# A new instruction order for three fused networks: first weight units in halves, fewer warm-up products, the passage to the third network opened

## The chip, the cores and the metric

The kernel runs on one core of a Trainium2 chip. The core has a matrix engine (TensorE, PE in the rows; PEld is its loading of the stationary operand), a vector engine (DVE), an activation engine (ACT), a general engine (POOL) and a queue for transfers (SP), each with its own instruction stream. They wait for each other by semaphores. The metric is the device time of one execution in microseconds, lower is better.

## The reference

Three networks follow each other. Everything is float32 with the weights given as 64-bit floats; B = 4, 8 heads, 576 positions, width 64.

```python
def _attn_ref(q, k, v):                       # landmark attention, m = 32
    q_lm = q.reshape(B, H, m, S // m, D).mean(axis=3)
    k_lm = k.reshape(B, H, m, S // m, D).mean(axis=3)
    A, Bm, C = sm(q, k_lm), sm(q_lm, k_lm), sm(q_lm, k)
    Z = Bm.T / (norm1(Bm) * norminf(Bm) + 1e-6)
    for _ in range(6):
        Z = 2 * Z - Z @ Bm @ Z
    return A @ Z @ C @ v
def _moe_ref(x, w1, w2, w3, w_out):           # 2304 tokens, 512 -> 1024 -> 1024 -> 512
    return ((x @ w1) * (x @ w2) @ w3) @ w_out
def _moe2_ref(x, w_in, w_out):                # 512 -> 2048 -> 512
    h = x @ w_in
    return (h * tanh(softplus(h))) @ w_out    # Mish
```

## The kernel before

**Attention** makes, for each of the four batches, landmark sums (DVE), small row-tiled score products on TensorE (32 or 64 rows of the array at a time, in one bank several side by side), the softmaxes and an iterated inverse.

**Second network.** w3 and w_out stand behind each other without anything between, so their product is made once, at the start: 16 units of w3 times 8 units of w_out, 64 products of two fp32 instructions each (line L349, "mm n x" is product x of unit w3n; it needs unit wo j of w_out with j = 2 (n % 4) + x // 2). A unit is 512 KB of 64-bit floats. Its load (L202) is issued on SP; then "da" takes the upper bits on ACT or DVE (L194, L196) and "db" joins them with the rest on DVE (L206), which gives 32-bit numbers. The other matmuls of the two networks are split into a high and a low part and done as three products each (`mm3`, L186 to L188). w1 and w2 are first multiplied with the landmark part ("m b s", L795, small products into the two-bank tile `pair`), and the result is split by ACT and DVE into M ("mh", "ml"). "xa" and "xb" are the two large products with it, six matmuls of 288 columns each, "xm" their product on DVE. Then "sh" and "sl" split the hidden rows into hs, "y u m" multiplies them with the made w3 times w_out, 24 matmuls of 288 columns, and "ye u m" copies the result out of its bank on ACT.

**Third network.** It runs in steps g = 0 to 23, each with a Strassen-like scheme of seven products, "Z0 g" to "Z6 g", six matmuls of 384 columns each into two banks in turn. They need the input y in several sums ("yh", "yl": high part by ACT, low part by DVE) and w_in in several sums ("zs" on DVE, "zh" on ACT, "zl" on DVE; stored by "zd"). S (L1293, ACT) copies Z0's bank, Q, R, C21, C22 and C12 (L1273, DVE) add up, E1, E2 and E3 are the Mish function on ACT in two forms (L1269, L1270), L1 to L3 the low part (DVE), and O0 to O3 the products with w_out. "wh", "wl" and "ws" split a unit of w_out for that and store it. "db 14", "wh 6" belong to unit 14, which is part 6 of w_out. The first use of the Mish function needs its table on ACT, one load (L1269).

**The order.** Nothing is scheduled by a program: the string `ORDER` lists every step by name (with @ENGINE where there is a choice), and `issue` walks through it and emits each step. So the order of the names is the order of the instructions on each engine, and a step waits behind everything ahead of it on its engine. A step's list of needed steps is only used to check the order and its slots; the semaphores come from the tiles that are read and written. Buffers are taken from pools (`raw`, `raw2` for the loaded units, the banks of PSUM in pool "w"). From g = 10 on the steps are emitted by loops that the change doesn't touch.

**Start.** Twenty products of a tile of ones with itself (L1395) go ahead of the string; they compute nothing that is used. L1273 to L1293 are in `z_ops`; L202 to L206 are `load`, `top_bits` and `join`.

Of the kernel before, what the change touches and what calls it, by code (L numbers as in the profile page):

```python
# [18 lines left out]
SPIN = 20  # L19
# [137 lines left out]
def kernel(  # L157
# [43 lines left out]
    def load(w, n):  # L201
        nc.sync.dma_start(out=w.bitcast(U16)[:, 1:2049], in_=wts[n].bitcast(U16))  # L202
# [75 lines left out]
    def got(key):  # L278
        pool, i = at[key]
        return pools[pool][i]  # L280
# [1194 lines left out]
```

## Time and profile before

| what | value |
|---|---|
| time, median of 3 runs | 706.01 us (705.64 to 706.74) |
| the profiled execution | 706.82 us |
| its span in the trace | 705.0 us |
| TensorE busy | 697.4 us, 5004 matmuls |
| VectorE (DVE) busy | 395.2 us |
| ScalarE (ACT) busy | 281.6 us |
| granted clock of TensorE | 1.00 |

The span is the time from the first to the last recorded instruction; the profiled execution's own time has 1.8 us around it. Busy times are sums of durations on one engine. Matmuls overlap, so the duration of one is longer than the distance to the next; where a price per matmul is needed it is the distance.

### The profile page before, as it was taken

The numbers are of one execution on the slowest core, as the hardware profiler recorded it, in microseconds if no ns is written. First come the engines' busy times: TensorE is split into PE (matmuls) and PEld (weight loads), VectorE is DVE, ScalarE is ACT, GpSimd is POOL, SyncE is SP. The second block draws the span as 40 slices with busy tenths as digits, with TensorE's granted clock in tenths as the row PEclk, the third lists the DMA queues.
The fourth block names the chain that finished last, engine by engine and source line by source line (L and its number), as shares of the span: only waits on it lengthen the run. The fifth ranks groups of instructions, "written<-read, shape, count | busy, mean of one in ns | idle before, by whom it ended". The sixth has DMA issues, their size and how long they took to land.

```text
span 705.0 us, 12344 instructions
## 1 busy us (share of the span) xinstructions
PE 697.4 (99%) x5004; PEld 594.3 (84%) x5004; DVE 395.2 (56%) x814; ACT 281.6 (40%) x644; POOL 27.8 (4%) x27
## 2 busy tenths in 40 slices
PE   9999999999999999999999999999999999999997
PEld 4445588888998999999898989898989988989896
DVE  5899787966446435766668667442234544222322
ACT  1355555536344326455454345522222442222222
POOL 0123011111000000000000000000000000000000
PEclk9999999999999999999999999999999999999999
DMA  9987895544042443554483766867544456555302
GB/s 352 383 293 258 267 343 183 171 150 120 17 150 80 153 172 120 195 208 170 151 323 136 274 232 275 299 236 285 210 186 165 165 213 219 204 214 207 152 2 89
DMA packets 36217, 141.38 MB, mean 201 GB/s; under 512 B 3648, under 2 KB 4032, under 8 KB 32576
## 3 DMA queue, kind: packets, MB, share of 16 engines
q1 hardware_dynamic: 36016, 140.46, 55.4%
q8 instruction: 39, 0.64, 0.4%
q14 instruction: 18, 0.15, 0.1%
q10 hardware_dynamic: 144, 0.13, 0.1%
HBM read 106.50 MB, written 34.08 MB: 199 GB/s over the span
## 4 chain that ended last, share of the span: by engine, by line
PE 97%; DVE 1%; ACT 1%; issue 0%; ACTq 0%
PE ps L186 27%; PE ps L187 27%; PE ps L188 27%; PE ps L349 8%; PE pair L795 2%; PE ps L604 1%; PE ps L410 1%; PE pair L1395 1%; PE ps L536 1%; PE ps L515 1%; ACT M L210 0%; DVE M L224 0%; PE pair L410 0%; DVE yH L224 0%; PE ps L517 0%
## 5 line engine op out<-in xcount | busy, mean ns | idle before, releaser
L187 PE MATMUL ps<-hs,W 128*128 128x288 f32 (+1 forms) x298 | 92.3, 310 | 0.0
L186 PE MATMUL ps<-hs,W 128*128 128x288 f32 (+1 forms) x298 | 92.3, 310 | 0.0
L188 PE MATMUL ps<-hs,W 128*128 128x288 f32 (+1 forms) x298 | 92.2, 309 | 0.0
L1273 DVE TENSOR_TENSOR hsb<-ps,zt 128x384 f32<-128x384 f32 x72 | 39.9, 557 | 86.7 <-PE ps L188 86.5
L1269 ACT ACTIVATE hsb<-hsb 128x768 f32<-128x768 f32 (+1 forms) x48 | 32.8, 684 | 114.8 <-DVE hsb L1273 114.8
L186 PE MATMUL ps<-AT,M 128*128 128x288 f32 x256 | 77.7, 304 | 0.1
L188 PE MATMUL ps<-AT,M 128*128 128x288 f32 x256 | 75.4, 295 | 0.0
L187 PE MATMUL ps<-AT,M 128*128 128x288 f32 x256 | 75.4, 294 | 0.0
L1273 DVE TENSOR_TENSOR zt<-ps,zt 128x384 f32<-128x384 f32 x48 | 26.7, 556 | 81.9 <-PE ps L188 76.5
L224 DVE TENSOR_TENSOR W<-hsb,W 128x384 fp32r<-128x384 f32 (+1 forms) x72 | 49.2, 687 | 17.4 <-ACT W L1270 17.4
L349 PE MATMUL ps<-wo,raw 128*128 128x512 f32 x128 | 58.5, 603 | 0.0
L188 PEld LDWEIGHTS ps<-hs,W 128*128 128x128 f32 x298 | 55.9, 188 | 1.8
L187 PEld LDWEIGHTS ps<-hs,W 128*128 128x128 f32 x298 | 56.1, 188 | 1.3
L186 PEld LDWEIGHTS ps<-hs,W 128*128 128x128 f32 x298 | 56.0, 188 | 1.3
L186 PEld LDWEIGHTS ps<-AT,M 128*128 128x128 f32 x256 | 48.0, 188 | 9.6 <-issue 5.0
L187 PEld LDWEIGHTS ps<-AT,M 128*128 128x128 f32 x256 | 48.1, 188 | 0.0
L188 PEld LDWEIGHTS ps<-AT,M 128*128 128x128 f32 x256 | 48.0, 188 | 0.0
L349 PEld LDWEIGHTS ps<-wo,raw 128*128 128x128 f32 x128 | 24.0, 196 | 25.4 <-issue 20.2
L210 ACT ACTIVATE a<-ps 128x288 f32<-128x288 f32 x64 | 25.6, 410 | 45.7 <-PE ps L188 45.4
L833 DVE TENSOR_TENSOR h<-a,ps 128x288 f32<-128x288 f32 x64 | 28.1, 450 | 26.0 <-ACT hs L210 9.8
L187 PE MATMUL ps<-yH,zw 128*128 128x384 f32 x120 | 40.3, 336 | 0.3 <-DVE yH L224 0.3
L187 PE MATMUL ps<-yH,hs 128*128 128x384 f32 x120 | 40.2, 335 | 0.0
(196 smaller groups left out, 1542.9 us busy)
## 6 DMA issues: line engine op xcount, KB each, us to landing
raw<-in_wts_dram SPq DMA_DIRECT2D x72, 512.0 KB, 4.6
zw<-zd SPq DMA_DIRECT2D x8, 1792.0 KB, 7.6
hs<-zd SPq DMA_DIRECT2D x8, 1792.0 KB, 7.3
zd<-zw SPq DMA_DIRECT2D x4, 1792.0 KB, 7.2
zd<-hs SPq DMA_DIRECT2D x4, 1792.0 KB, 7.5
wy<-wod SPq DMA_DIRECT2D x12, 512.0 KB, 6.7
W<-wod SPq DMA_DIRECT2D x10, 512.0 KB, 7.1
k<-in_kT_dram SPq DMA_DIRECT2D x8, 576.0 KB, 5.7
```

The costliest lines, as they stand in the source:

```text
L186: T.matmul(out=o, lhsT=lh, rhs=rh, start=first, stop=False, skip_group_check=partial)
L187: T.matmul(out=o, lhsT=lh, rhs=rl, start=False, stop=False, skip_group_check=partial)
L188: T.matmul(out=o, lhsT=ll, rhs=rh, start=False, stop=last, skip_group_check=partial)
L210: S.activation(o, x, ACTF.Copy)
L224: (G if e == "POOL" else V).tensor_tensor(o, x, f32(hi), op=ALU.subtract)
L349: T.matmul(out=got(f"acc{i}"), lhsT=f32(middle(got(f"w3{n}"))[:, o:o + 128]), rhs=WO0[j // 4][:, j % 4], start=j == 0, stop=j == 7)
L410: T.matmul(out=mine(f"{key}{g}{hf}")[32 * i:32 * i + 32, 0:HALF], lhsT=st[lm][r, p, :], rhs=st[x][r, p, hf * HALF:(hf + 1) * HALF], start= ...
L515: T.transpose(out=mine(f"ct{g}0")[:, ck * 128:(ck + 1) * 128], in_=x[:, ck * 128:(ck + 1) * 128], identity=idn)
L795: T.matmul(out=got("p" + key)[32 * i:32 * i + 32, c, :], lhsT=LT[r, b, 2 * c + par, :], rhs=w12(f"w{bp}{s}{2 * c + par}")[r], start=True, ...
L833: V.tensor_tensor(hslice(u, s), got("s" + key), got("b" + key)[:, 0:HALF], op=ALU.mult)
L1269: S.activation(e, src_, ACTF.Mish)
L1273: V.tensor_tensor(o, x, y, op=ALU.add)
```

## The change

Five fewer warm-up products. Units w30 and w34 of w3 are loaded, and decoded, in two halves of 256 columns each, and a product waits for its half only. Z0 of g = 0 may stand ahead of the last y products (its wait for all of them is taken out of the list; S gets the wait for all xm, and C and E of g = 0 get the wait for all y). The string `ORDER` is another one throughout.

```diff
-SPIN = 20
+SPIN = 15
+
+HALVED = (0, 4)
...
-    "ld wo0,da wo0@ACT,db wo0,ld w34,da w34@DVE,ld w30,da w30@ACT,db w34,mm 4 0,mm 4 1,db w30,mm 0 1,ld wo1,da wo1@DVE,db wo1,"
...
+    "ld w34a,ld wo0,da wo0@ACT,ld w30a,db wo0,dA w30a@DVE,ld w30b,dA w30b@DVE,dB w30a,mm 0 0,dB w30b,ld wo1,mm 0 1,"
...
-    def top_bits(e, w, u):
-        o, i = u.bitcast(F16).rearrange("p (n w) -> p n w", w=2)[..., 1], w.bitcast(BF16)[:, 2:2050].rearrange("p (n w) -> p n w", w=4)[..., 2]
+    def top_bits(e, w, u, c=slice(0, 512)):
+        o, i = u.bitcast(F16).rearrange("p (n w) -> p n w", w=2)[:, c, 1], w.bitcast(BF16)[:, 2:2050].rearrange("p (n w) -> p n w", w=4)[:, c, 2]
...
-    def load(w, n):
-        nc.sync.dma_start(out=w.bitcast(U16)[:, 1:2049], in_=wts[n].bitcast(U16))
+    def load(w, n, c=slice(0, 512)):
+        a, z = 4 * c.start, 4 * c.stop
+        nc.sync.dma_start(out=w.bitcast(U16)[:, 1 + a:1 + z], in_=wts[n].bitcast(U16)[:, a:z])
...
+    def decode_halves(u, n, raw, take):
+        for i, h in enumerate("ab"):
+            c = slice(256 * i, 256 * i + 256)
+            step(f"ld {u}{h}", "SP", [f"ld {u}a"], lambda e, c=c: load(raw(), n, c), take if i == 0 else ())
+            step(f"dA {u}{h}", ("ACT", "DVE"), [f"ld {u}{h}"] + ([f"dA {u}a"] if i else []), lambda e, c=c: top_bits(e, raw(), got("u" + u), c),
+                 () if i else {"u" + u: "u"})
+            step(f"dB {u}{h}", "DVE", [f"dA {u}{h}"], lambda e, c=c: join(raw(), got("u" + u), None, c), (), ["u" + u])
...
-        step(me, "PE", [f"db w3{n}", f"db wo{j}"] + chain(f"mm{i}", me), mm,
+        step(me, "PE", [f"dB w3{n}{'ab'[a]}" if n in HALVED else f"db w3{n}", f"db wo{j}"] + chain(f"mm{i}", me), mm,
...
+    all_xm = [f"xm {b} {s} {h}" for b in (2, 3) for s in range(NS) for h in range(2)]
...
-            ("Z0", "PE", z_wait(0, f"C12 {p}", *all_y), lambda e: z_mm(g, 0)),
-            ("S", "ACT", [f"Z0 {g}", f"C21 {p}"], lambda e: S.activation(zt(0), z_bank(0), ACTF.Copy)),
+            ("Z0", "PE", z_wait(0, f"C12 {p}"), lambda e: z_mm(g, 0)),
+            ("S", "ACT", [f"Z0 {g}", f"C21 {p}"] + all_xm, lambda e: S.activation(zt(0), z_bank(0), ACTF.Copy)),
...
-        return [(f"{n} {p if n[0] == 'O' else g}", e, w, fn) for n, e, w, fn in table]
+        first = all_y if g == 0 else []
+        return [(f"{n} {p if n[0] == 'O' else g}", e, w + first * (n[0] in "CE"), fn) for n, e, w, fn in table]
```

The transfer queue SP at the start of the program, before: raw is the landing place of a unit, 128x2048 a whole one (16-bit columns), k and q a half of a batch's keys or queries, idn the identity matrix. By `ORDER` the first units are wo0, w34, w30, wo1, w31, wo2, w35, wo3.

```order
L202 DMA raw_73<-in_wts_dram 128x2048 x3
L202 DMA raw<-in_wts_dram 128x2048 x4
L202 DMA raw_73<-in_wts_dram 128x2048
L386 DMA k<-in_kT_dram 128x2x576 x2
L386 DMA q<-in_qT_dram 128x2x576 x2
L324 DMA idn<-in_ident_dram 128x128
L202 DMA raw_73<-in_wts_dram 128x2048 x3
```

And after the change, where the units are w34a, wo0, w30a, w30b, wo1, w34b, wo2, w31, w35, wo3, and after q and k w32, wo4 and w36:

```order
L206 DMA raw_73<-in_wts_dram 128x1024
L206 DMA raw_73<-in_wts_dram 128x2048
L206 DMA raw_73<-in_wts_dram 128x1024 x2
L206 DMA raw<-in_wts_dram 128x2048
L206 DMA raw_73<-in_wts_dram 128x1024
L206 DMA raw<-in_wts_dram 128x2048 x3
L206 DMA raw_73<-in_wts_dram 128x2048
L398 DMA q<-in_qT_dram 128x2x576
L398 DMA k<-in_kT_dram 128x2x576 x2
L398 DMA q<-in_qT_dram 128x2x576
L206 DMA raw_73<-in_wts_dram 128x2048 x3
```

Half a unit now stands ahead of wo0, the four halves of q and k come in another sequence, and the identity matrix is loaded later; w32 and wo4 still follow right behind q and k.

ACT at the passage from y to Z, before: y<-ps is ye (the copy of a y product out of its bank), yW and yH are yh, zt<-ps_78 is S 0, and the last two rows are E1 0. [waits PE_49] marks a wait for TensorE.

```order
L210 ACTIVATE y_3126<-ps_81 128x288
L210 ACTIVATE yH_3539<-sums 128x768 [waits Activation_49]
L210 ACTIVATE y_3432<-ps_2867 128x288 [waits PE_49]
L210 ACTIVATE yW_3546<-y_2140 128x768 [waits DMAHW7_49,DMAHW3_49,Activation_49]
L210 ACTIVATE yH_3575<-sums 128x768 [waits DVE_49,Activation_49]
L210 ACTIVATE y_3432<-ps_2866 128x288 [waits PE_49]
L210 ACTIVATE yW_3583<-y_2140 128x768 [waits DMAHW1_49,DMAHW0_49,Activation_49]
L210 ACTIVATE y_3432<-ps_77 128x288
L1293 ACTIVATE zt<-ps_78 128x384 [waits PE_49]
L1269 ACT_TABLE_LOAD
L1269 ACTIVATE hsb<-ps_78 128x384 [waits PE_49]
L1270 ACTIVATE W_64<-ps_78 128x384
```

And after: S 0 is the first row, y_3457<-ps_82 in the fourth is ye 7 3, the two hs<-sums are zh6 1 and zh4 1, W_65<-raw is wh 6, and the two y behind it ye 7 2 and ye 7 1.

```order
L1306 ACTIVATE zt<-ps_78 128x384 [waits PE_49]
L214 ACTIVATE yW_3529<-y_2151 128x768 [waits DMAHW7_49,DMAHW0_49,Activation_49]
L214 ACTIVATE y_3149<-ps_81 128x288
L214 ACTIVATE y_3457<-ps_82 128x288 [waits PE_49]
L214 ACTIVATE hs_1953<-sums 128x256 [waits DVE_49]
L214 ACTIVATE hs_1953<-sums 128x256
L214 ACTIVATE W_65<-raw 128x512 [waits DMAHW1_49,DVE_49]
L214 ACTIVATE y_3457<-ps_79 128x288
L214 ACTIVATE y_3457<-ps_77 128x288
L1282 ACT_TABLE_LOAD
L1282 ACTIVATE hsb<-ps_78 128x384 [waits PE_49]
L1283 ACTIVATE W_64<-ps_78 128x384
```

Before, the table's load follows S 0 directly. After, eight rows lie between the two, among them ye 7 3. On TensorE, Z0 0 now stands between y 7 0 and y 7 1, and Z1 0 to Z3 0 follow y 7 3, then Z4 0.

## Rows read from the trace of the kernel before

**Rows 1.** The page: span, and busy time of each engine.

```profile
span 705.0 us, 12344 instructions
...
PE 697.4 (99%) x5004; PEld 594.3 (84%) x5004; DVE 395.2 (56%) x814; ACT 281.6 (40%) x644; POOL 27.8 (4%) x27
```

**Rows 2.** Waits of TensorE: engine, line, releaser, us in total, times, longest.

```profile
PE pair L1395 <- DVE ones L1393: 1.5, 1, 1.5
PE ps L186 <- DVE hsb L1273: 0.7, 1, 0.7
...
PE pair L795 <- DVE M L224: 0.5, 2, 0.3
```

**Rows 3.** Windows: us, busy time (instructions) per engine, TensorE clock, DMA share, GB/s.

```profile
20.00:40.00 20.00, 20.00 (x118) 8.72 (x119) 18.28 (x39) 10.01 (x24) 3.70 (x3) 1.00 0.96 356
250.00:300.00 50.00, 50.00 (x377) 50.00 (x376) 29.43 (x67) 22.98 (x59) 0.00 (x0) 1.00 0.45 153
```

**Rows 4.** Timeline of the start: start us, us, engine, line, operation, idle before, releaser.

```profile
4.36 0.78 ACT L194 ACTIVATE top<-raw 128x512 f16<-128x512 bf16 x1 [2.35 <-DMA raw<-in_wts_dram]
...
5.17 0.69 DVE L206 SCALAR_TENSOR_TENSOR wo<-raw,top 128x512 int32<-128x512 int32 x1 [3.77 <-ACT top L194]
...
5.70 1.91 PEld L1395 LDWEIGHTS <-ones 128*128 128x128 bf16 x9 [0.28 <-issue]
5.78 0.45 DVE L196 TENSOR_SCALAR top<-raw 128x512 f16<-128x512 bf16 x1
...
7.45 0.78 ACT L194 ACTIVATE top<-raw 128x512 f16<-128x512 bf16 x1 [2.32 <-DMA raw<-in_wts_dram]
...
7.93 11.37 PE L349 MATMUL ps<-wo,raw 128*128 128x512 f32 x26
...
21.41 0.78 ACT L194 ACTIVATE top<-raw 128x512 f16<-128x512 bf16 x1 [13.17 <-DMA raw<-in_wts_dram]
...
22.68 0.79 ACT L194 ACTIVATE top<-raw 128x512 f16<-128x512 bf16 x1 [0.49 <-DMA raw<-in_wts_dram]
...
23.53 0.68 DVE L206 SCALAR_TENSOR_TENSOR wo<-raw,top 128x512 int32<-128x512 int32 x1
...
24.26 0.31 PEld L349 LDWEIGHTS ps<-wo,raw 128*128 128x128 f32 x2 [0.69 <-DVE wo L206]
```

**Rows 5.** Chain of waits, 58 to 70 us: start us, us, what.

```profile
60.82 1.92 PE ps L349 x4
...
62.99 5.36 PE ps L349 x12
```

**Rows 6.** Chain of waits, 118 to 123.5 us.

```profile
121.15 0.61 ACT M L210
...
121.78 0.70 DVE M L224
...
122.52 1.04 PE pair L795 x9
```

**Rows 7.** Timeline of the passage from y to Z.

```profile
321.34 0.41 ACT L210 ACTIVATE y<-ps 128x288 f32<-128x288 f32 x1 [1.32 <-PE ps L188]
...
321.64 0.84 ACT L210 ACTIVATE yW<-y 128x768 fp32r<-128x768 f32 x1
...
324.34 0.34 PE L186 MATMUL ps<-yW,zw 128*128 128x384 f32 x1
...
325.58 0.49 ACT L1293 ACTIVATE zt<-ps 128x384 f32<-128x384 f32 x1 [2.80 <-PE ps L188]
...
326.09 1.28 ACT L1269 ACT_TABLE_LOAD   x1
...
327.67 0.49 ACT L1269 ACTIVATE hsb<-ps 128x384 f32<-128x384 f32 x1 [0.29 <-PE ps L188]
...
328.59 0.19 PEld L186 LDWEIGHTS ps<-yH,zw 128*128 128x128 f32 x1 [0.23 <-ACT W L1270]
```

**Rows 8.** Groups of ACT by form: busy us, mean ns, idle before, releasers.

```profile
L210 ACT ACTIVATE W<-raw 128x512 fp32r<-128x512 f32 x3 | 2.0, 665 | 6.0 <-DVE raw L206 6.0
```

More of the change, by code (lines that the diff above doesn't have):

```diff
@@ L199, in middle, with join @@
         return w[:, 1:1025].rearrange("p (n w) -> p n w", w=2)[..., 0]
-    def load(w, n):
-        nc.sync.dma_start(out=w.bitcast(U16)[:, 1:2049], in_=wts[n].bitcast(U16))
-    def join(w, u, to=None):
+    def load(w, n, c=slice(0, 512)):
+        a, z = 4 * c.start, 4 * c.stop
+        nc.sync.dma_start(out=w.bitcast(U16)[:, 1 + a:1 + z], in_=wts[n].bitcast(U16)[:, a:z])
+    def join(w, u, to=None, c=slice(0, 512)):
         to = middle(w) if to is None else to.bitcast(I32)
-        V.scalar_tensor_tensor(to, middle(w), 13, u, op0=ALU.logical_shift_right, op1=ALU.bitwise_or)
+        V.scalar_tensor_tensor(to[:, c], middle(w)[:, c], 13, u[:, c], op0=ALU.logical_shift_right, op1=ALU.bitwise_or)
     def copy(e, o, x):
@@ L337, in add_w3 @@
         u = f"w3{n}"
-        decode(u, 8 + n, lambda: got(u), {u: raw_pool(u)})
+        (decode_halves if n in HALVED else decode)(u, 8 + n, lambda: got(u), {u: raw_pool(u)})
         for i in range(4):
```

245 rows, old and new, of the table ORDER are left out of this document.

## The prediction

> **What bounds the kernel now.** I read the busy shares first, then the waits of TensorE, then stretches of the start, of the middle and of the places that the new order rewrites. The reader is to see that TensorE is busy 697.4 of 705.0 us [rows 1], that its waits are few and short (1.5 us before the warm-up, then tenths) [rows 2], and that it runs without a gap at full clock both while the weights are loaded and in the middle of the kernel: 20.00 of 20.00 us busy between 20 and 40 us, 50.00 of 50.00 between 250 and 300 us with 377 matmuls, .133 us each for 288 columns [rows 3]. So the time is a fixed number of matmuls plus the places where TensorE stands still or changes its kind of product. An edit counts only if it removes matmuls, removes such a place or makes a new one. The other engines have 40 to 56% and matter only where TensorE ends up waiting for them.
>
> **The base of the sum.** The profiled execution took 706.82 us, 1.8 us more than its span of 705.0. The sum is made against it. It lies .8 us above the median of the runs, 706.01; I carry the sum over to the median as a difference.
>
> **Start: fewer spins, halves, new order of loads.** The last spins stand .21 us apart (nine loads in 1.91 us [rows 4]), so five fewer free TensorE 1.06 us earlier, at 6.87 us instead of 7.93 [rows 4]. Whether the first product is ready then is a walk along the loads. Two units of 512 KB are decoded 1.27 us apart when their decoding waits for the transfers (21.41 and 22.68 [rows 4]), and the stream stays that full (DMA .96 [rows 3]). In the kernel before wo0 stands first in the queue and its decoding starts at 4.36. Now half a unit, w34a, stands ahead of it, so it starts at 4.36 + .64 = 5.00; ACT takes .78, DVE's join .69, which ends at 6.50. DVE's queue then holds the upper bits of w30a and of w30b and then the join of w30a. A decoding of 128x256 is not in the trace: it lies between half and the whole of .45 and .69 [rows 4]. Three of them end between 7.3 and 8.1; I take 7.6, nearer the half, since these shapes are paid by columns elsewhere. The first product starts at about 7.6 instead of 7.93, and TensorE waits .7 us behind its last spin. The product mm 0 2 then needs wo1, with 3.5 units to its end in the queue: the third unit's decoding started at 7.45 before [rows 4], so wo1's starts at about 8.1, its join ends at 9.7, two products (.86 us each) end at 9.3, and .4 us of the gain is given back.
>
> What decides the start is the end of it. In both kernels 16 products can be made before one needs wo4, and in both ten units and four halves of q and k lead up to wo4 in the queue. Before, ACT decodes it at 22.68, DVE joins it at 23.53, and TensorE's load waits for that until 24.26 [rows 4]. The new kernel has the same bytes ahead of it (the small identity matrix is moved behind, some tenths), the same two steps on the same engines, and comes there some tenths earlier only to wait. I take 0. Bounds: -1.1 (all of the five spins is kept, because other products lie ready) and +.7 (the small transfers or the halves' decoding hold wo1 or wo4 up).
>
> A rule of the Trainium skill speaks against the halves. The row first: back-to-back units of 512 KB come 1.27 us apart [rows 4], about 410 GB/s, so transfers of that size already fill the stream. The page DMA: Bandwidth & Descriptors, section Bandwidth, asks for at least 1 MiB per transfer to have 75% of the peak and gives 341 GB/s for 1 MB. By that rule units and halves alike would be slow; the row disagrees for a queue with many transfers in flight, no row shows 256 KB on loads, and by the rule the sum would move by the four halves, at most to the +.7 that the bound has anyway.
>
> **Changes of the kind of product.** Between plain products stand groups of small row-tiled ones (scores, landmark products, the m products). What such an island costs beyond its own matmuls is read from two pieces of the chain: four w3 instructions behind a group take 1.92 us, twelve behind another 5.36 [rows 5]. The slope is 3.44/8 = .43 each, and the rest, 1.92 - 4 x .43 = .20, belongs to the change out of the group and back. In the program order of TensorE I count 30 such islands before and 26 after. Four times .20 is -.8; the new order makes some other changes more often (transposes next to small products), for which I give back .2: -.6, between -.8 and -.2.
>
> **Waits for the M tiles.** TensorE's m products wait twice for DVE's M, .5 us in sum [rows 2]: m 1 2 at 122.52 us, and m 3 2 later, each time behind the chain ACT M, DVE M, ACT M, DVE M (.61 and .70 each, and TensorE .04 behind it [rows 6]), because too few x products stand between. That chain is about 2.7 us long (twice .61 and .70, and the gaps). In the new order m 1 2 has four more x products and a bp ahead of it (some 3.5 us) and m 3 2 has eight x products instead of four, so both chains end before TensorE arrives: -.5, between -.8 and 0, the zero for a wait that reappears at another m.
>
> **The passage from y to Z.** This is the largest term, and it is a loss. Before, y 7 3 is followed by Z0 at 324.34, S on ACT runs at 325.58, the Mish table is loaded at 326.09 for 1.28 us, E1 starts at 327.67 and Z4, which waits for the bank that E1 reads, at 328.59 [rows 7]. A Z product is six matmuls of 384 columns, .174 each by the .133 of 288 columns [rows 3]; four of them from 324.34 end at 328.52, so Z4 loses .07. The table is hidden, since ACT has nothing else to do there.
>
> In the new order Z0 0 stands ahead of y 7 1, S 0 is early, but the table isn't: ACT's queue has ye 7 3, which waits for y 7 3's end (call it T0), and behind it zh6 1, zh4 1, wh 6, ye 7 2, ye 7 1 and only then the table. ye 7 3 starts at T0 + .20 (S stands .20 behind Z0's six matmuls [rows 7]). Copies of this size follow each other in .30 (321.34, 321.64 [rows 7]) though each lasts .41; wh 6 copies 128x512, .665 us [rows 8], .56 with the same overlap. Five times .30 and .56 are 2.06: table at T0 + 2.26, E1 at T0 + 3.54, and Z4 .92 behind E1's start as before (327.67 to 328.59): T0 + 4.46. TensorE has only Z1, Z2, Z3 to do in that time, 18 x .174 = 3.13. It waits 1.33, less the .07 of before: +1.3. With whole durations (.41, .665) the queue takes 2.7 and the loss is +1.9; with another .30 between the table and E1, as the rows allow (327.67 - 326.09 is 1.58), +2.2. The other end is -.1: ACT's six copies run before T0, or the table early. I take +1.3. Nothing behind it gives it back: Z0 1 already waits for the end of a chain that starts with Z6, and moves with it.
>
> The Trainium skill makes more of the table. The page ScalarE: Activation LUTs, section What ACT_TABLE_LOAD costs, has 1283 ns and another 1380 ns of drain, 2.66 us for each switch. The trace agrees with the first and not with the second: E1 starts 1.58 us after the load's start [rows 7], and there it waited for TensorE. By the rule Z4 would lose another 1.3 us and the sum would be +1.5.
>
> **Everything else** keeps its instructions: the Strassen-like products, the O products and the tail. The longest wait in there, .7 us for hsb at L1273 [rows 2], has the same neighbours. 0, plus or minus .5 for single fetch stalls.
>
> **Sum.** 0 - .6 - .5 + 1.3 + 0 = +.2: 707.0 for an execution like the profiled one, 706.2 for a median like 706.01. A difference under .2% (1.4 us) can't be told from none in this kernel; so the forecast is no change.
>
> **Rivals.**
> - The table costs nothing (the passage is neutral): Z4's bank is free otherwise, or ACT runs the six copies while y 7 3 still computes. For it: ACT is idle most of that stretch. Against it: ye 7 3 reads what y 7 3 writes and stands first. +.2 - 1.3 = -1.1: 704.9.
> - The five spins are won whole: for it, TensorE waits nowhere else between 20 and 40 us [rows 3], so an earlier start might be kept if the products behind 24 us are not bound by loads. Against it, the wait at 24.26. -1.1 more: 705.1. With the first rival too: 703.8.
> - Slower: unit 14 is late. wh 6 stands before the table and needs unit 14 joined on DVE, whose load was only issued behind the stores ws 5 and ws 3 in SP's queue, and which DVE decodes (.45 and .69) behind other differences. It decides from the point where the join ends later than T0 + 1.1 (ACT's turn for wh 6); from there each microsecond is paid in full, since table, E1 and Z4 stand behind it. At T0 + 3 it costs 1.9: 708.1. Against it: y 7 1 to y 7 3 give some 9.6 us for the load.
> - The first weights starve TensorE (halves cost as much as wholes): +.7 to +1, 707.0.
> - The table holds ACT longer than its row: if ACT needed as long again behind the load (1.28) before E1 can run, Z4 would lose another 1.3: 707.5. Against it, E1 runs .30 behind the load's end at 327.37 [rows 7]. That is the drain that the Trainium skill's page ScalarE: Activation LUTs speaks of.
>
> **Chances.** Forecast .50 (705.2 to 707.2 of its own), table free .14, spins kept .11, both .05, unit 14 late .10, starved start .06, table held longer .04. Faster by over .2% (under 704.6): both, about two fifths of the two single gains, and the forecast's lower tail: .26. Slower (over 707.4): most of unit 14, the table held longer, a part of the starved start and the forecast's upper tail: .18. The rest, .56, within. The range of 8 in 10 reaches to 703.9, nearly the two gains together, and to 707.8, short of the late unit.
>
> **What would show it.** First product at 7.5 to 7.7 and the product with wo4 at 24.2 to 24.3, or earlier (then the spins are won). No wait at m 1 2 and m 3 2. The table's load starts 2.2 us after the last matmul of y 7 3, and TensorE waits 1.2 to 1.6 us ahead of Z4, released by ACT W. If the load starts earlier, or Z4 doesn't wait, the first rival holds; if ACT waits for DVE's raw ahead of wh 6, the third. It is wrong if the time moves by over 1.4 us, or if the rest of the body, which I set at 0, has gained or lost more than half a microsecond.

## The result and the profile after

The changed kernel takes 714.22 us (median of 5 runs, 713.93 to 716.82) against 706.01 (705.43 to 706.74): a ratio of 1.0124, with 95% interval 1.0105 to 1.0143 (the ratios here and below are taken over all fast runs and not from the medians, so they differ a little from the medians' quotient). It is slower by 8.2 us. The prediction, 706.2 us with a range of 703.9 to 707.8, was wrong. The profiled execution took 714.84 us, 8.0 more than that of before.

The page of the changed kernel, to be read against [rows 1]: span, and busy time of each engine.

```profile
span 713.0 us, 12348 instructions
...
PE 699.3 (98%) x4999; PEld 594.8 (83%) x4999; DVE 394.6 (55%) x812; ACT 285.7 (40%) x651; POOL 26.0 (4%) x25
```

TensorE has five matmuls fewer, the spins, and is busy 1.9 us longer. So idle time is not the whole loss: some matmuls became slower. The waits of TensorE after the change stand against [rows 2] (engine, tile, line, releaser, us in total, times, longest):

```profile
PE ps L548 <- issue: 2.8, 1, 2.8
PE ps L361 <- DVE raw L210: 1.9, 2, 1.5
PE ps L189 <- ACT W L1283: 1.3, 1, 1.3
PE ps L189 <- DVE hsb L1286: 0.7, 1, 0.7
PE ps L189 <- DVE csm L520: 0.5, 1, 0.5
PE ps L189 <- DVE h L845: 0.3, 1, 0.3
PE ps L616 <- DVE py L673: 0.2, 1, 0.2
```

The two waits for M are gone. New at the top is one of 2.8 us with no releaser but "issue": TensorE waited for nothing that the profile shows. The kernel before has one wait of this kind, which is much shorter:

```profile
PE ps L410 <- issue: 0.6, 1, 0.6
```

The row of 1.3 us is Z4 waiting for ACT. The lines are renumbered: L349 is now L361, L186 to L188 are L189 to L191, L206 is L210, L1273 is L1286, L1269 is L1282.

**Where the 8 us lie.** Two instructions that exist in both kernels, the load for the product with wo4 and that of Z4, cut the span in three. TensorE's busy time between them is from the windows of both traces.

| stretch | before | after | difference |
|---|---|---|---|
| to the product with wo4 | 24.26 | 25.58 | +1.3 |
| from there to Z4 0 | 304.33, busy 302.95 | 311.31, busy 305.58 | +4.4 idle, +2.6 busy |
| from Z4 0 to the end | 376.4 | 376.1 | -0.3 |

The windows of the middle stretch, before and after (us, busy time and instructions of PE, PEld, DVE, ACT, POOL, then clock, DMA share, GB/s):

```profile
24.26:328.59 304.33, 302.95 (x3057) 251.39 (x3057) 208.05 (x474) 145.84 (x387) 26.62 (x22) 1.00 0.54 183
25.58:336.89 311.31, 305.58 (x3056) 252.50 (x3056) 207.79 (x472) 148.28 (x395) 24.86 (x20) 0.99 0.51 176
```

The idle 4.4 us are the stall (2.8, against .6 of the same kind before), the gap at Z4 (1.45 against .08 by the distance of the matmuls' starts; the row of 1.3 counts from the end of the last one), and small waits that came for those that went. Of the 2.6 us busy, 1.8 are worked out below; .8 I could not place.

**The start.** Two pieces of the timeline (start us, us, engine, line, operation, idle before with its releaser), against [rows 4].

```profile
5.40 0.77 ACT L197 ACTIVATE top<-raw 128x512 f16<-128x512 bf16 x1 [3.39 <-DMA raw<-in_wts_dram]
...
7.52 0.31 DVE L199 TENSOR_SCALAR top<-raw 128x256 f16<-128x256 bf16 x1 [0.61 <-DMA raw<-in_wts_dram]
...
8.39 0.75 DVE L210 SCALAR_TENSOR_TENSOR raw<-raw,top 128x256 int32<-128x256 int32 x2
8.87 0.31 PEld L361 LDWEIGHTS ps<-wo,raw 128*128 128x128 f32 x2 [2.03 <-DVE raw L210]
...
23.92 0.79 ACT L197 ACTIVATE top<-raw 128x512 f16<-128x512 bf16 x1 [0.47 <-DMA raw<-in_wts_dram]
...
25.58 0.31 PEld L361 LDWEIGHTS ps<-wo,raw 128*128 128x128 f32 x2 [0.40 <-DVE wo L210]
```

The first product starts at 8.87 us, not at 7.93 as before nor at the 7.6 that was worked out. Its wait is for transfers: w30a's decoding starts at 7.52, although 256 KB and 512 KB stood ahead of it and wo0's decoding had started at 5.40. The whole stream is then behind: wo4's decoding starts at 23.92 instead of 22.68. This place differs between executions: in nine profiled ones with the new start (this one, e1, e2, e3, e5, e7, e8, e9, e13 below) the product with wo4 starts at 24.73 to 25.58, mean 25.11, and in six with the old start (before, e6, e10, e11, e12, e14) at 23.90 to 24.88, mean 24.31. So the start costs about .8 on average, and 1.3 between the two executions compared here. The first product starts at 7.70 to 8.87 (mean 8.32) in the nine and at 7.38 to 8.69 (mean 8.04) in the six, so the five spins less don't bring it forward.

**The stall and what follows it.** Windows of the changed kernel, and the chain of waits there.

```profile
60.00:64.00 4.00, 3.85 (x140) 2.26 (x141) 3.51 (x9) 2.67 (x9) 2.99 (x3) 1.00 1.02 360
64.00:67.00 3.00, 0.25 (x5) 0.16 (x4) 2.93 (x8) 0.00 (x0) 0.48 (x1) 1.00 0.69 276
67.00:70.00 3.00, 3.00 (x7) 1.49 (x6) 1.29 (x6) 2.91 (x11) 0.00 (x0) 0.65 0.04 10
70.00:73.00 3.00, 3.00 (x25) 1.26 (x24) 2.90 (x9) 0.86 (x3) 0.00 (x0) 0.78 0.00 0
68.00:71.00 3.00, 3.00 (x5) 1.31 (x4) 1.93 (x7) 2.72 (x10) 0.00 (x0) 0.50 0.00 0
```

```profile
63.14 0.82 PE ps L548 x36
63.96 2.79 issue
66.75 0.30 PE ps L548 x4
67.05 5.34 PE ps L361 x8
```

TensorE stops in the middle of a group of 40 small products (L548, "cv"), so no operand is missing: 36 of the same group had just run. Ahead of the stop stand 140 matmuls in 4 us (13 in the four before); the new order puts five groups of small ones (16, 40, 32, 16 and 40) in a row. Behind it the granted clock averages .65 and then .78 in windows of 3 us. These are no levels of their own: from 68 to 71 us it is .50, the lower of the two levels (1.2 and 2.4 GHz), and the averages mix it with 1.00, the upper one. The eight w3 matmuls there take 5.34 us. At the .43 of [rows 5] and one change of kind, .1, they would take 3.55: 1.8 us for the clock.

The page's row of the queue that carries instructions (packets, MB, share), then the data queue's row from 60.3 to 63.9 us, where the instruction queue has none, and the instruction queue's from 63.9 to 66.8:

```profile
q8 instruction: 39, 0.64, 0.4%
```

```profile
q1 hardware_dynamic: 532, 1.29, 97.9%
```

```profile
q8 instruction: 1, 0.02, 2.1%
```

39 transfers of 16,384 bytes fit the 10,000 instructions of TensorE, 256 to a block: a matmul and its load are two, so a block lasts 128 matmuls. At .43 us each that is 55 us; the small ones use it up in 3.7 us (from 60.26, which is 256 instructions ahead of the stop, to 63.96). From 60.3 to 63.9 no block came, while the data transfers filled the engines to 97.9%; the next one started at 64.30, 4.0 us after the block before it was used up, and TensorE went on 1.5 us after its end. The Trainium skill's page Runtime: NRT & Kernel Launch, section Instruction fetch mechanics, names such a FIFO with blocks of 16 KiB that the sequencer fetches on a queue of its own, and calls the cost of a crossing "mostly hidden". The size agrees with the row of 39 packets; that it is hidden does not hold here, with 2.79 us.

That such a stop is a wait for instructions is also shown by its place. Counted over all kept traces there are 21 stops over .15 us with no releaser but "issue" in the middle of the kernel, in both orders, with either start and in the joins below. Each stands behind the 961st, the 1473rd or the 1729th recorded instruction of TensorE, which are 512 and 256 apart, whatever product is there; and each ends 1.2 to 1.6 us after the end of a block's transfer. The kernel before has 109 small products in a row at 57.5 us, less than a block, and doesn't stop there; its stop of .6 us is behind the 1473rd instruction, in a run of 229.

**The passage from y to Z**, the chain of waits of the changed kernel against [rows 7]:

```profile
332.48 0.03 ACT y L214
...
332.79 0.71 ACT hs L214 x2
333.50 0.56 ACT W L214
334.06 0.60 ACT y L214 x2
...
334.68 1.28 ACT L1282
...
335.97 0.49 ACT hsb L1282
...
336.89 0.45 PE ps L189
```

TensorE goes on from y 7 3 to Z1 at 332.29, the T0 of the prediction's sum. ye 7 3 starts .19 us later (.20 was worked out), the table's load 2.39 (2.26) and Z4 4.60 (4.46). This term was right step by step; the .13 are the two copies to hs, .71 instead of .60. E1 starts 1.29 us behind the start of the load of 1.28, and it had nothing else to wait for, since Z2 was long done. So no drain of 1.38 us follows the load, which the Trainium skill's page ScalarE: Activation LUTs, section What ACT_TABLE_LOAD costs, adds to it.

### The profile page after: what moved, and what is told of

It reads as the page before. It is cut to its first block, busy times and chain, and to the rows that moved or that the text cites. A ratio compares the mean times of both kernels' runs of the same rounds, so it can differ in the third digit from the quotient of the medians.

```text
span 713.0 us, 12348 instructions
## 1 busy us (share of the span) xinstructions
PE 699.3 (98%) x4999; PEld 594.8 (83%) x4999; DVE 394.6 (55%) x812; ACT 285.7 (40%) x651; POOL 26.0 (4%) x25
## 4 chain that ended last, share of the span: by engine, by line
PE 91%; DMA 3%; DVE 2%; ACT 2%; issue 1%; SPq 1%; ACTq 0%; DVEq 0%
PE ps L189 27%; PE ps L191 27%; PE ps L190 27%; PE ps L361 5%; DMA raw<-in_wts_dram 3%; PE pair L807 2%; PE ps L616 1%; PE ps L422 1%; PE ps L548 1%; SPq L206 1%; DVE raw L210 1%; PE ps L527 0%; DVE M L228 0%; ACT M L214 0%; DVE mx L443 0%
## 5 line engine op out<-in xcount | busy, mean ns | idle before, releaser
L189 PE MATMUL ps<-hs,W 128*128 128x288 f32 (+1 forms) x298 | 92.5, 310 | 0.0
L191 PE MATMUL ps<-hs,W 128*128 128x288 f32 (+1 forms) x298 | 92.2, 310 | 0.0
L1286 DVE TENSOR_TENSOR hsb<-ps,zt 128x384 f32<-128x384 f32 x72 | 39.7, 556 | 86.0 <-PE ps L191 86.0
L1282 ACT ACTIVATE hsb<-hsb 128x768 f32<-128x768 f32 (+1 forms) x48 | 32.9, 685 | 120.6 <-DVE hsb L1286 120.6
L189 PE MATMUL ps<-AT,M 128*128 128x288 f32 x256 | 78.1, 305 | 1.0 <-DVE csm L520 0.5
L191 PE MATMUL ps<-AT,M 128*128 128x288 f32 x256 | 75.6, 295 | 0.0
L1286 DVE TENSOR_TENSOR zt<-ps,zt 128x384 f32<-128x384 f32 x48 | 26.7, 556 | 73.1 <-PE ps L191 70.5
L361 PE MATMUL ps<-wo,raw 128*128 128x512 f32 x128 | 59.7, 616 | 2.5 <-DVE raw L210 1.9
L189 PEld LDWEIGHTS ps<-hs,W 128*128 128x128 f32 x298 | 56.1, 188 | 3.0 <-ACT a L214 0.8
L191 PEld LDWEIGHTS ps<-hs,W 128*128 128x128 f32 x298 | 56.0, 188 | 1.7
L189 PEld LDWEIGHTS ps<-AT,M 128*128 128x128 f32 x256 | 48.1, 188 | 9.3 <-issue 5.4
L361 PEld LDWEIGHTS ps<-wo,raw 128*128 128x128 f32 x128 | 24.7, 201 | 31.7 <-issue 23.2
L191 PEld LDWEIGHTS ps<-AT,M 128*128 128x128 f32 x256 | 48.1, 188 | 0.2 <-DVE M L228 0.2
L197 ACT ACTIVATE top<-raw 128x512 f16<-128x512 bf16 x38 | 29.3, 785 | 34.5 <-DMA raw<-in_wts_dram 30.1
```

Of the source, the lines that this page charges most:

```text
L189: T.matmul(out=o, lhsT=lh, rhs=rh, start=first, stop=False, skip_group_check=partial)
L191: T.matmul(out=o, lhsT=ll, rhs=rh, start=False, stop=last, skip_group_check=partial)
L197: S.activation(o, i, ACTF.Copy)
L361: T.matmul(out=got(f"acc{i}"), lhsT=f32(middle(got(f"w3{n}"))[:, o:o + 128]), rhs=WO0[j // 4][:, j % 4], start=j == 0, stop=j == 7)
L1282: S.activation(e, src_, ACTF.Mish)
L1286: V.tensor_tensor(o, x, y, op=ALU.add)
```

## Experiments

Four kinds: on the stall, on the start, on the passage, and joins of the two orders. "Before" in each batch lay between 705.95 and 706.70 us.

### The stall of the instruction stream

**e2_spread** puts plain products between the groups of small ones.

```diff
-... cs1 1, cm01 1, ... cex01 1, mm 12 0, mm 12 2, mm 12 1, ...
+... cs1 1, mm 12 0, mm 12 2, cm01 1, ... cex01 1, mm 12 1, ...
```

> The changed kernel with the products mm 12 0 and mm 12 2 (1.7 us of TensorE's work, eight instructions with their loads) moved from behind the run of small products (nm4, cv0, cs0, cs1, nm5, cv1: 144 matmuls in 3.8 us) into its middle, between cs1 1 and nm5 0. Theory (TensorE's instructions run out in a run of small products, since they are used up faster than the next block of them is fetched): the stall of 2.8 us at 64 us shrinks to about 1 us or less, and with it the .65 and .78 of granted clock behind it: 710 to 712. Rival (the stall is a wait for data or a fetch that comes at a fixed place of the program): the stall stays at 2 us or more, 713.5 to 714.5.

Measured: 712.41 us, ratio 1.0086 (1.0073 to 1.0099), below the interval of the changed kernel; 1.8 us less by the medians, .4 over the range that was expected. Its windows, as above:

```profile
60.00:64.00 4.00, 3.99 (x92) 2.00 (x89) 2.80 (x6) 2.13 (x8) 2.43 (x3) 1.00 1.00 377
64.00:67.00 3.00, 1.76 (x59) 0.89 (x57) 2.04 (x6) 0.39 (x2) 0.23 (x1) 1.00 0.58 227
67.00:70.00 3.00, 2.94 (x26) 1.65 (x27) 2.90 (x11) 2.65 (x10) 0.00 (x0) 1.00 0.08 7
```

The stall is gone and the clock is 1.00 throughout. Of the 4.6 us only 1.8 are won, because other waits took part of the place (two fetch stalls, behind the 1473rd and the 1729th instruction, and two waits on ACT and DVE in the moved group):

```profile
PE ps L527 <- issue: 0.9, 1, 0.9
PE ps L361 <- ACT cv L557: 0.8, 1, 0.8
PE ps L616 <- DVE py L673: 0.8, 1, 0.8
PE ps L422 <- issue: 0.7, 1, 0.7
```

**e9_notraffic** keeps the order and takes the data transfers away there: of w313, w314, w315 and the keys of batch 2 only a few columns are loaded, so what is computed from them isn't the reference's.

```diff
-        step(f"ld {u}", "SP", [], lambda e: load(raw(), n), take)
+        step(f"ld {u}", "SP", [], lambda e: load(raw(), n, slice(0, 4) if u in ("w313", "w314", "w315") else slice(0, 512)), take)
-                nc.sync.dma_start(out=st[x][:, 2 * i:2 * i + 2, :], in_=src[:, 2 * i:2 * i + 2, :])
+                s = slice(0, 8) if (x, b) == ("k", 2) else slice(0, S_LEN); nc.sync.dma_start(out=st[x][:, 2 * i:2 * i + 2, s], in_=src[:, 2 * i:2 * i + 2, s])
```

> The changed kernel with small transfers in place of the loads of the units w313, w314 and w315 and of the keys of batch 2 (four columns or eight positions of each, so those products use old data); every instruction and wait stays. So from about 59 us the transfer queue is nearly empty while TensorE runs through the small products at 60 to 64 us. Theory (TensorE's next block of instructions is fetched by the same transfer engines and comes late because they are full): the block's transfer starts within 2 us of the 336th matmul (4.1 us in the changed kernel), the stall at 64 us is .8 us or less, the clock stays at 1.00, and the time is 709 to 711.5. Rival (the block is late whatever the engines carry, since 256 instructions are used up in 3.8 us): a stall of 1.6 us or more, as in all executions so far, and 713 to 715.

Measured: 710.88 us, ratio 1.0066 (1.0041 to 1.0091), 3.3 us below the changed kernel. The same small products in the same order, with free transfer engines: windows, and the queues from 60.1 to 63.4.

```profile
60.00:64.00 4.00, 4.00 (x145) 2.48 (x146) 3.51 (x8) 2.13 (x8) 2.47 (x3) 1.00 0.08 8
64.00:67.00 3.00, 3.00 (x8) 1.37 (x8) 2.93 (x9) 1.86 (x6) 0.33 (x1) 1.00 0.03 5
```

```profile
q1 hardware_dynamic: 398, 0.01, 6.5%
q8 instruction: 1, 0.02, 1.8%
```

145 matmuls in 4.00 us without a gap: the block's transfer started at 61.11, 1.0 us after the one before was used up (60.12), instead of 4.0. So both are needed, many small matmuls in a row and full transfer engines, and it is the second that makes the block late. The time won is less than 4.6, as in e2: two waits in the list of this run, for py (.7 instead of .2) and a fetch stall at another place (.5, L527), take 1.0 of it.

**e3_light** moves loads out of that stretch.

```diff
-... ld w313, ... wsm 3, lk1 2, da w313, db w313, ... mm 12 3, ...
+... mm 12 3, wsm 3, lk1 2, ld w313, da w313, db w313, ...
```

> The changed kernel with the loads of lk1 2 and w313 (and their decoding, and the store wsm 3) moved from ahead of the products of unit w312 to behind them, so that about 1.3 MB less is in the transfer queue while TensorE runs through the small products at 60 to 64 us. Theory (the block of instructions comes late because it is fetched through the transfer engines, which are full with loads, share 1.02 at 60 to 64 us): the stall of 2.8 us falls to 1 us or less, 709.5 to 711.5. Rival (the fetch takes its time whatever else is transferred): the stall stays, and w313's products wait for their unit too, 714 to 715.5.

Measured: 714.56 us, ratio 1.0123 (1.0098 to 1.0148). Inconclusive: the transfers did not become fewer (DMA share 1.04 from 56 to 60 us and .95 from 60 to 64, against .87 and 1.02 in the changed kernel). The store wsm 3 and the keys' load no longer stand on SP behind the load of w313, which is issued only at 58.0 there, so the keys' load came earlier, at 52.2 instead of 58.9. The stall was 1.6 us there and .6 at another place.

**e7_first** and **e6_rest** join the two orders: e7 has the new order to the step `swap` and the old one behind it, e6 the old one to `m 2 0`, with whole units and twenty spins, and the new one behind.

```diff
 e7: after's order to "swap", then
-... after's rest
+... before's rest
 e6: after's rest, and ahead of it
-... after's order to "m 2 0"
+... before's order to "m 2 0"
```

> The reverse: the start and the attention of the changed kernel (its order as far as the step swap, halves, 15 warm-up products), and from there on the order of the kernel before. Theory: all of the loss but the passage's 1.3 us: 712.5 to 713.5 in the median, with the stall of 1.5 to 3 us at 64 us and a granted clock under 1.00 behind it in most executions, and no wait at Z4 0 over .2 us. Rival (the stall depends on the whole program, by where blocks of instructions end): under 710.5.

> The start and the attention of the kernel before (its order as far as the step m 2 0, whole units, 20 warm-up products), and from there on the order of the changed kernel. Theory (what is lost lies in the start, the run of small products with the fetch stall and the clock behind it, and 1.3 us in the passage): only the passage is lost, 707.3, within .5, and the times spread as little as before's. Rival (the changed order loses in the second network too, after 160 us): over 708.5.

Measured: e7 713.46 us, ratio 1.0097 (1.0079 to 1.0114), with a stall of 2.0 us at L548, one of 1.1 at L527 and no wait at Z4. Its runs at 710.09 and 711.28 had a mean clock of 1.0, those from 713.4 up .997 to .998. e6 708.92 us, ratio 1.0046 (1.0034 to 1.0058), with the wait of 1.3 for W at Z4 and one of 1.4 for ACT that the join itself makes. Less that, the second half costs 1.5 us and the first 7.4, together 8.9 for the 8.2 measured: so most of the loss lies ahead of the step `swap`, and with it ahead of the third network.

### The start

**e8_start** has the new start alone, halves and fifteen spins, to `mm 1 3`; **e4_whole** is the changed kernel with whole units.

```diff
 e8: after's order to "mm 1 3", then
-... after's rest
+... before's rest
 e4:
-HALVED = (0, 4)
+HALVED = ()
-... ld w34a, ld wo0, ld w30a, ld w30b, ld wo1, ld w34b, ld wo2, ld w31, ld w35, ld wo3
+... ld wo0, ld w30, ld wo1, ld w34, ld wo2, ld w31, ld w35, ld wo3
```

> Only the start of the changed kernel (its order as far as mm 1 3, halves, 15 warm-up products), then the order of the kernel before. Theory (the start loses .6 to 1.3 us, since the first half unit takes as long as a whole one to land and the stream up to wo4 comes later): the product with wo4 starts at 24.7 to 25.6 instead of 24.26, and the time is 706.6 to 707.4. Rival (loads bind the start and not the products, so the start costs nothing; all of the loss is behind 40 us): 706.0 within .3.

> The changed kernel with units w30 and w34 loaded and decoded whole, in the sequence wo0, w30, wo1, w34, wo2, w31, w35, wo3; everything else as in the changed kernel. Theory (the transfers of 256 KB at the very start are slow, so the whole stream up to wo4 comes 1.2 us late): wo0 lands at 4.3, wo4 lands at 22.6 instead of 23.84, the first product starts at 7.6 to 8.0 instead of 8.87, and the time falls by 1 to 1.5 us, to about 712.9. Rival (the start is bound by the decoding on DVE or by the products' order): the stream is earlier but the products with wo4 are not, and the time stays at 714.2 within .5.

Measured: e8 707.15 us (11 runs), ratio 1.0022 (1.0011 to 1.0032): +1.1 us for the start alone. In its timeline the product with wo4 is late by the same amount, at the upper end of its nine:

```profile
25.39 0.31 PEld L361 LDWEIGHTS ps<-wo,raw 128*128 128x128 f32 x2 [0.79 <-DVE wo L210]
```

e4 714.23 us, ratio 1.0110 (1.0095 to 1.0125), not told from the changed kernel. Its first product starts at 7.33, and the one with wo4 at 24.75, .36 ahead of the mean with halves but within their range; its third unit landed as late as 8.00 us. The stall was 2.5 us here. One part of the .8 is seen in the landings of all kept traces: the first half unit lands at 4.06 to 4.20 us in the nine with halves, the first whole one at 4.27 to 4.46 in the seven without. So half the bytes come some .2 earlier, where .64 was worked out, and about .4 is lost there each time. For the rest the runs don't settle whether it belongs to the halves.

**e14_start** is e13 (below) with the old start, whole units and twenty spins, to `mm 1 3`.

```diff
-SPIN = 15
+SPIN = 20
-HALVED = (0, 4)
+HALVED = ()
-... after's order to "mm 1 3"
+... before's order to "mm 1 3"
```

> The kernel of e13_spread_table with the start of the kernel before too (its order as far as mm 1 3, whole units, 20 warm-up products). Theory (the start costs .6 to 1.3 us): the product with wo4 starts at 24.0 to 24.6, and the time is .6 to 1.3 under that of e13_spread_table, about 710.2. Rival (what is gained at the start is lost again at the run of small products, whose block of instructions comes when the engines are full): the same time as e13_spread_table within .3.

Measured: 713.27 us, ratio 1.0100 (1.0080 to 1.0121), no faster than e13. The product with wo4 stands at 24.51 (24.73 in e13), but TensorE's stream now stalls for 1.9 us at 89.26, where e13 had none that long, and the granted clock falls behind it (the chain's row, and a window):

```profile
89.26 1.90 issue
```

```profile
93.00:96.00 3.00, 3.00 (x24) 2.14 (x10) 1.38 (x3) 1.04 (x3) 0.00 (x0) 0.50 1.07 327
```

e13 stops for .3 us behind the second of four products of line L527, at its 1729th instruction. In e14 five more matmuls stand ahead, and the same 1729th instruction is five matmuls earlier in the order, among x products. So what was won at the start was lost again at a fetch, as the rival said.

### The passage

**e1_table**, **e5_spread_table** (on top of e2), and **e13_spread_table** (on top of e2) put the table's load and E1 first on ACT, and what stood ahead of it at three places behind.

```diff
 e1:
-... ye 7 3, ... zh6 1, ... zh4 1, wh 6, wl 6, R 0, ye 7 2, ye 7 1, zl6 1, E1 0, Z4 0, ...
+... R 0, E1 0, ye 7 3, zh6 1, zh4 1, wh 6, wl 6, ye 7 2, ye 7 1, zl6 1, Z4 0, ...
 e5:
+... R 0, E1 0, ye 7 3, ye 7 2, ye 7 1, Z4 0, ... E2 0, zh6 1, zh4 1, wh 6, wl 6, zl6 1, Z6 0, zl0 1, C12 0, Z0 1, ...
 e13:
+... R 0, E1 0, ye 7 3, ye 7 2, ye 7 1, Z4 0, ... E2 0, Z6 0, zl0 1, C12 0, zh6 1, zh4 1, wh 6, wl 6, zl6 1, Z0 1, ...
```

> The changed kernel with ye 7 3, zh6 1, zh4 1, wh 6, wl 6, ye 7 2, ye 7 1 and zl6 1 moved behind E1 0 in the order, so that on ACT the Mish table's load stands ahead of ye 7 3 and can run beside y 7 1 to y 7 3. Theory (the passage costs 1.3 us because the table's load waits behind ye 7 3): the wait ahead of Z4, 1.45 us in the changed kernel, falls under .2 us and the time by 1.2 to 1.4, to about 712.9. Rival (the wait is given back later, or the banks that ye 7 3 frees are needed at once): the wait moves to another Z or O product and the time stays at 714.2 within .4.

Measured: 715.54 us, ratio 1.0124 (1.0104 to 1.0143): no gain, as its rival said, and 1.3 us above the rival's time; the three runs above 715 us have a mean clock of .994 to .995. Z4 no longer waits, but wl 6 now stands ahead of C22 0 on DVE, and Z6 0 waits 1.1 us for that; the row for hsb is 1.1 larger than in the changed kernel.

```profile
PE ps L189 <- DVE hsb L1286: 1.8, 2, 1.1
```

> The kernel of e2_spread (two products of unit w312 in the middle of the small products) with the table's load moved too, in another way than in e1_table: ye 7 3, ye 7 2 and ye 7 1 stand behind E1 0, and zh6 1, zh4 1, wh 6, wl 6 and zl6 1 only behind E2 0, so that DVE's C22 0 does not stand behind the difference wl 6 that waits for ACT. Theory (the passage costs 1.3 us, and in e1_table the wait only moved because wl 6 came ahead of C22 0 on DVE): neither Z4 0 nor Z6 0 waits over .2 us, and the time is 1.3 under e2_spread's 712.4: 711.1, within .4. Rival (the wait returns at a third place): 712.4 within .3.

Measured: 716.72 us, ratio 1.0156 (1.0143 to 1.0170), slower still. Here wl 6 stands ahead of C12 0, for which Z0 1 waits. The chain of waits, the wait itself, and windows:

```profile
340.43 0.69 DVE W L228
...
341.79 0.48 DVE hsb L1286
...
343.00 0.32 PE ps L190
```

```profile
PE ps L189 <- DVE hsb L1286: 4.2, 1, 4.2
```

```profile
342.00:345.00 3.00, 2.69 (x8) 2.69 (x9) 2.97 (x7) 1.25 (x3) 0.00 (x0) 0.50 0.18 76
345.00:348.00 3.00, 3.00 (x9) 2.64 (x9) 1.43 (x4) 1.11 (x3) 0.00 (x0) 0.50 1.08 421
```

After 4.2 us of waiting the clock is .50, the lower level, for the 6 us of the two windows. Matmuls of 384 columns come .32 us apart instead of .174 and those of 512 columns .43 instead of .23: twelve of the one and four of the other stand there, so the clock costs an estimated 2.6 us on top of the wait.

> The kernel of e2_spread with the passage put in order as in e11_passage_fixed (ye 7 3, ye 7 2, ye 7 1 behind E1 0; zh6 1, zh4 1, wh 6, wl 6, zl6 1 behind C12 0). Theory (the passage costs 1.3 us, and nothing else in it is disturbed now): no wait over .3 us at Z4 0 and Z6 0, .8 at Z0 1 as in the kernel before, and 711.1, within .5, against 712.4 of e2_spread. Rival (a wait of 1 us or more comes back among the O products or at Z0 1): 712.4 or more.

Measured: 712.19 us (median of five; a sixth run took 1381 us and is left out), ratio 1.0081 (1.0061 to 1.0100). Z4, Z6 and Z0 1 don't wait any more than before the change, but an O product does, for a copy on DVE that the moved work pushed back:

```profile
343.07 0.44 PE L189 MATMUL ps<-yH,hs 128*128 128x384 f32 x1 [0.57 <-DVE zt L1286]
```

So about .6 of the 1.45 us comes back, and the time (5.5 over its batch's before, against 6.4 for e2, with intervals of the ratios that overlap) doesn't tell the rest from nothing.

**e10_passage** and **e11_passage_fixed** try the same without the first half: the old order to `y 7 0`, with whole units and twenty spins, then the new one, in e11 with the arrangement of e13.

```diff
 e10:
-... after's order to "y 7 0"
+... before's order to "y 7 0"
 e11: e10, and
+... R 0, E1 0, ye 7 3, ye 7 2, ye 7 1, Z4 0, ... C12 0, zh6 1, zh4 1, wh 6, wl 6, zl6 1, Z0 1, ...
```

> The kernel before up to y 7 0 (whole units, 20 warm-up products), and from there on the order of the changed kernel: the passage and the third network alone. Theory: the table's load stands behind ye 7 3 and Z4 0 waits 1.3 us more than before: 707.3, within .4. Rival (in a kernel that loses nothing earlier the passage is hidden or made up for later): 706.0 within .3.

> The kernel of e10_passage with ye 7 3, ye 7 2 and ye 7 1 behind E1 0 and zh6 1, zh4 1, wh 6, wl 6 and zl6 1 behind C12 0, so that neither the table's load nor C22 0 or C12 0 stands behind a step that waits for ACT's copies (in e5_spread_table C12 0 stood behind wl 6, and Z0 1 waited 4.2 us). Theory: no wait over .2 us at Z4 0 and Z6 0, and Z0 1 waits .8 as before: 706.0, within .4. Rival (the copies are late for something else): a wait of 1 us or more at O3 0, O0 0 or Z4 1, 707 or more.

Measured: 710.41 us, ratio 1.0057 (1.0038 to 1.0075), and 710.93, ratio 1.0064 (1.0044 to 1.0085). The wait at Z4 is 1.45 us in e10, as expected, and none in e11. But the join itself makes Z0 0 wait for its inputs, 1.6 us in e10 and 1.9 in e11 for ACT and .6 more for DVE, and the granted clock is .50 for some 3 us behind it; the times of both are inconclusive.

### A try to keep the gain

**e12_best** takes the one part that did what it should, the later m products, into the kernel before.

```diff
-... m 1 2, mh 1 4, ... xa 0 4 1, ... m 3 2, mh 3 4, ml 3 4, ... xa 2 4 0, ...
+... xa 0 4 1, m 1 2, mh 1 4, ... xa 2 4 0, m 3 2, mh 3 4, ml 3 4, ...
```

> The kernel before with m 1 2 and mh 1 4 two x products later, and m 3 2, mh 3 4 and ml 3 4 one x product later, nothing else. Theory (TensorE waits .38 and .45 us for DVE's M there, and the chain of M is covered by more x products): both waits go, 705.2, within .3 of that. Rival (the waits move to the next x products, which need the M that is now made later): 706.0 within .3.

Measured: 708.10 us (12 runs), ratio 1.0024 (1.0012 to 1.0036): slower. The wait of TensorE for M falls from .5 to .2 us, but it now waits .7 for ACT's cv in the same stretch, and some .3 more at three other places. From one and the same product to another there (119.81 to 141.81 us before, 119.04 to 142.78 here) it takes 1.7 us longer. No version beat the kernel before.

## Why the prediction was wrong

- **"Everything else ... 0, plus or minus .5 for single fetch stalls": this step failed.** It was mis-sized by about 4 us: a stall of 2.8 against .6 before, and 1.8 for the clock behind it. The new order puts five groups of small products in a row, more than one block of instructions, and [rows 3] showed how full the transfer engines are while weights come (DMA .96); the two were never put together. e9 and e2 show the cause from both sides, and the places of the stops (961, 1473, 1729) show that it is the fetch. The bound of .5 is near the one stall in the trace of before (.6), which says how the old order lay to its blocks and nothing of another order.
- **Start, "I take 0", with +.7 as the bound: mis-sized.** +1.3 between the two executions, .8 on average over fifteen, +1.1 in the time of e8. The walk along the loads took half the bytes for half the time (.64 for w34a) and no hole in the stream. The transfers went otherwise: w34a, half a unit, landed at 4.09 us, a whole first unit in the kernel before at 4.27, and w30a only at 7.49. Half a unit's decoding takes .31 and .42 us, more than half of .45 and .69. The rival "starved start" (+.7 to +1) was right here, and nothing of the five spins was won.
- **Islands, "-.6": about right, and too small to show.** Between the two cuts of the table the traces have 30 groups of small products before and 26 after, as was counted. Going in costs .09 us (.52 instead of .43 behind a w3 matmul), coming out about .11. An estimate: with the median distance for every matmul by its kind and its neighbours' the middle stretch adds up to 286.7 us before and 286.2 after, .5 less.
- **M waits, "-.5": right in place, and taken back.** Both rows are gone. Waits of .5, .3 and .2 us on DVE stand in the list instead, at other steps; that they come from the removal is not shown.
- **Passage, "+1.3": right**, in the trace, to .1 us (1.45 less .08), and in each step. That the rival with the late unit didn't come is shown by wh 6, which starts right behind zh4 1. The table held ACT no longer than its load (E1 starts 1.29 us behind the load's start), so the rival of the longer table failed. But the passage's worth in time is not shown: where the wait was undone it came back elsewhere in part (e13) or in whole (e1).
- The terms found in the two traces, start, passage, stall and clock, are 1.3 + 1.4 + 2.2 + 1.8 = 6.7 of the 8.0 us between the two executions; .8 is busy time without a place (with the .5 less for the groups it is more), and the rest small waits.
- **Open:** why the clock falls behind some stalls and not behind others. The length of the stop alone doesn't decide it. In the profiled runs it fell after 2.8 us in the changed kernel, 4.2 in e5, 1.9 in e14, and 1.6 and 1.9 with .6 more in e10 and e11, but not after 2.5 in e4, 2.0 in e7, 1.8 in e1 or 1.6 in e3, although other runs of e4 and e1 took 1 to 5 us longer than the profiled one. That this is also why the changed kernel's variants spread more (e3 from 711.56 to 718.45) than the kernel before is likely: in e7 the two fastest runs are those with a clock of 1.0.

## What to carry to other kernels

Where a new order puts many short matmuls in a row, count them against the blocks in which the instructions arrive, and look at what the transfer engines do in that stretch: a stall with no releaser in the middle of a group of equal products is the sign. One such stall in the trace of before gives the place of all block ends in this kernel: count TensorE's instructions from it in steps of 256, back and forth, and see which products the new order puts there. In this kernel, whose bound engine is 99% busy, single waits could not be taken out one by one at their traced price; after each removal here waits stood at other places. A step put ahead of a table's load delays everything behind that load on its engine, and the wait that follows could be read from the kernel before to a tenth of a microsecond; what it is worth in time was not shown.

## What the runs showed of the hardware

- The transfer of a block of TensorE's instructions started 4.0 us after the block before it was used up with the transfer engines 97.9% full, 1.0 us with them 6.5% full (e9). The price was 2.79 us once.
- The 21 stops of this kind in the kept traces stand behind TensorE's 961st, 1473rd or 1729th instruction, 256 or 512 apart, and end 1.2 to 1.6 us after a block's transfer. Five matmuls more ahead (e14) moved the stop by five matmuls in the order.
- The granted clock after a stop in the middle of the kernel: .50 from 68 to 71 us behind 2.8 us (1.8 us lost), .50 from 93 to 96 us behind 1.9 us in e14, .50 from 342 to 348 us behind 4.2 us in e5 (some 2.6 lost); 1.00 throughout behind 2.5 us in e4.
- ACT's table load holds ACT for its 1.28 us and no longer.
- At the start, the first 256 KB landed at 4.06 to 4.20 us in nine executions, the first 512 KB at 4.27 to 4.46 in seven; and the same start of a program differs by .9 us between executions.
